# Opening loads of a spectral-filter, soft-MoE and Mish kernel: half of x on another queue, and fewer filler products

## The chip, the cores and the metric

One core of one Trainium2 chip runs the whole program. The metric is device time of one execution in microseconds (us), the median of several runs. The engines are TensorE (PE; its weight loads are listed as PEld), VectorE (DVE), ScalarE (ACT), GpSimd (POOL) and SyncE (SP). Transfers are issued by SP, ACT or POOL, each on a queue of its own (in the profile's queue table q1 is SP's, q10 ACT's, q0 POOL's), and all queues share the core's 16 DMA engines.

## What is computed

Input x is 8 sequences of 3072 rows of 256 floats. All arithmetic is float32.

```python
X = np.fft.rfft(x, axis=1)
Yr = Xr @ w_r - Xi @ w_i + b_r          # same for Yi with b_i
Yr = sign(Yr) * max(|Yr| - 0.01, 0)      # same for Yi
x = np.fft.irfft(Yr + 1j * Yi, n=3072, axis=1).reshape(8 * 3072, 256)
logits = x @ phi                          # 32 slots, 8 experts of 4
d = softmax(logits, axis=0); c = softmax(logits, axis=1)
slot_out = experts(d.T @ x)               # relu(. @ w1) @ w2 for each expert
x = c @ slot_out
h = x @ w_in
out = (h * tanh(softplus(h))) @ w_out     # Mish gate
```

## The kernel before

The program has two parts. The first, up to about 720 us, does the spectral filter and the routing for the 8 sequences (b = 0 to 7) one after another; the second does the experts and the dense Mish layer. The Fourier transform of 3072 points is split into two stages of matrix products (64 by 48 points). For b = 1 to 7 the first stage (`stage1`, L239) takes tiles `xc` of x, and its result goes through DRAM (`sdr`) and back for the second stage (`stage2`, L269). Sequence 0 is the opening and goes another way, so that nothing has to wait for DRAM: all of x[0] is loaded into one tile `x0` of 128 partitions (`load_x0`, L187 to L192), and `first(c)` for c = 0 to 3 (L194 to L211) does the first stage for 64 of the 256 columns at a time and turns the result with a DVE transpose (`bt`, L211) into the tile that `stage2` reads.

`load_x0(c)` is called for two column halves, c = 0 and 1. Each call issues four transfers: r = 0, 1 (12 of 24 rows of a partition) and h = 0, 1 (partitions 0 to 63, the lower ones, and 64 to 127, the upper ones). So x[0] comes in eight pieces of 384 KB, each of 64 partitions times 12 rows of 512 bytes. SP issues the four lower pieces, ACT the four upper ones. `first(0)` and `first(1)` read only the four pieces of c = 0, `first(2)` and `first(3)` only those of c = 1. In each, the products take lower and upper partitions in turn, so the first product needs both lower pieces and the second one both upper pieces.

The order of the work is written by hand: `at(pos, fn, ...)` puts a function at a place, and all are run in the order of their places. The opening is: `setup` (the loads, L139 to L154), 46 filler products (`fill`, L560, 64 by 64 by 64 on the constant tile `f64`, whose result nobody reads), `first(0)` and `first(1)`, 28 filler products more, `first(2)` and `first(3)`, then `load_c` and the `xc` loads of b = 1 on SP's queue, `weights("a")`, and stages of k = 0, 1, ... Each filler and each other float32 product shows as two MATMUL instructions in the profile.

`setup` issues besides x: the constant `f64` (32 KB, ACT), the first quarter of a table of cosines `tall` (432 KB, SP), the two filter matrices into `wst` (256 KB each, ACT), and, on POOL's queue, two biases (`bias`, 1 KB each, in runs of 4 bytes) and the slot vectors phi (`ph`, 32 KB, in runs of 128 bytes). `wst` is first read by `weights("a")` on ACT (L170), `bias` by `biases` on DVE (L176).

Which semaphore a transfer uses is dealt out by the framework: transfers of SP and ACT share eight of them in turn (DMAHW0 to DMAHW7 in the order listings below), and a ninth transfer waits, on its issuing queue, until the one that used the same semaphore last has landed. POOL's transfers have semaphores of their own (DMASW).

Of the kernel before, what the change touches and what calls it, by code (L numbers as in the profile page):

```python
# [70 lines left out]
def body(ctx, tc, x, w_r, w_i, b_r, b_i, phi, w1, w2, w_in, w_out, cbig, ct, out, dbg=None, stop=False):  # L71
    nc = tc.nc
# [4 lines left out]
    def at(pos, fn, *a):  # L77
        items.append((round(pos, 4), len(items), fn, a))
# [47 lines left out]
    ph = wp.tile([128, 2, NS], F32, name="ph")  # L126
    bias = wp.tile([128, 2, 2], F32, name="bias")
# [6 lines left out]
    x_t, b_t, xh_t, xl_t, yt_t, y_t, pt_t, k1_t = {}, {}, {}, {}, {}, {}, {}, {}  # L134
# [4 lines left out]
    def setup():  # L139
        nc.scalar.preload_act_table_set("natural_log_exp_and_others")  # L140
        nc.scalar.dma_start(out=f64, in_=cbig[:, 416:480])
        wst = ytp.tile([128, 6, D], F32, tag="yt", name="wst")
        k1_t["w"] = wst
        x_t[0] = opx.tile([128, 2, N2, 128], F32, name="x0")
        for c in range(2):
            load_x0(c)
        load_t(0, 0)
        nc.scalar.dma_start(out=wst[:, 0:2], in_=w_r.rearrange("(h p) e -> p h e", p=128))
        nc.scalar.dma_start(out=wst[:, 2:4], in_=w_i.rearrange("(h p) e -> p h e", p=128))
        for i, src in ((0, b_r), (1, b_i)):  # L150
            nc.gpsimd.dma_start(out=bias[:, i], in_=src.rearrange("(h p) -> p h", p=128))
        nc.gpsimd.dma_start(out=ph, in_=phi.rearrange("(h p) e -> p h e", p=128))
        nc.vector.memset(ones32, 1.0)
        x_t["bt"] = op0.tile([96, 16, D, 2], F32, name="bt0")  # L154

# [26 lines left out]
    def load_t(i, g):  # L182
        w = 8 * (96 if i else 144)
        o = NP * 144 * i + g * w
        nc.sync.dma_start(out=tall[:, o:o + w], in_=ct[:, o:o + w])

    def load_x0(c):  # L187
        src = x[0].rearrange("(p h n) d -> h p n d", h=2, n=N2)
        for r in range(2):
            for h in range(2):  # L190
                (nc.scalar if h else nc.sync).dma_start(out=x_t[0][64 * h:64 * h + 64, c, 12 * r:12 * r + 12],
                                                        in_=src[h][:, 12 * r:12 * r + 12, 128 * c:128 * c + 128])  # L192

    def first(c):  # L194
# [454 lines left out]
    def load_c0():  # L649
        for r in range(4):  # L650
            for j, n in ((0, 6), (1, 2)):
                nc.sync.dma_start(out=c0[32 * r:32 * r + 32, 6 * j:6 * j + n].bitcast(F32).rearrange("s i t -> s (i t)"),
                                  in_=c_d[0][r % 2][j][:, 0:n].rearrange("s i t -> s (i t)"))

    at(-9, setup)
    at(12.05, load_c0)
    at(-5.5, fill, 46)
    at(-0.84, biases)
    at(-4.6, weights, "a")
    at(-0.86, weights, "b")  # L660
    at(-0.85, weights, "c")
    at(-4.85, fill, 28)
    for c in range(4):
        at(-5 + 0.1 * c, first, c)
    at(-4.28, load_c)
# [486 lines left out]
```

## Time and profile before

| what | value |
|---|---|
| time, median of 3 runs | 1822.76 us (1821.73 to 1824.0) |
| profiled execution | 1821.0 us |
| its span, first to last instruction | 1819.1 us |
| PE busy | 1796.6 us, 99% of the span |
| DVE busy | 1498.4 us, 82% |
| ACT busy | 1373.1 us, 75% |
| POOL busy | 265.8 us, 15% |
| granted TensorE clock, mean | 1.000 |

The table shows that PE is busy nearly all the time. The change lies in the first 30 us of the span only, and there the views to read are those that put events in order of time: the chain of work that ended last, the timelines of the engines, the issues of transfers with their time to landing, and the stretches with the rate at which bytes moved.

### The profile page before, as it was taken

What the parts mean: (1) busy time and instruction counts of PE and PEld (TensorE: products, weight loads), DVE (VectorE), ACT (ScalarE), POOL (GpSimd) and SP (SyncE); (2) the same over time, 40 slices, a digit from 0 to 9 for tenths busy, and PEclk for the clock granted to TensorE, in tenths of its full rate; (3) what the DMA queues carried; (4) which work ended last, traced back from release to release, by engine and by line L of the source; (5) the groups of instructions that cost most, each with busy time, mean ns of one, the idle gap of its engine ahead of it and who ended that gap; (6) DMA issues with size and microseconds to landing.
All of it is one profiled execution on the core that took longest, in us unless ns stands there. A gap on an engine that the chain in (4) does not pass through costs nothing.

```text
span 1819.1 us, 32257 instructions
## 1 busy us (share of the span) xinstructions
PE 1796.6 (99%) x12522; PEld 1548.0 (85%) x12522; DVE 1498.4 (82%) x2157; ACT 1373.1 (75%) x2232; POOL 265.8 (15%) x342
## 2 busy tenths in 40 slices
PE   9999999999998999999999999999999999999998
PEld 6878788787886688888888888888888888888887
DVE  5477776766766599999999999999999999999997
ACT  4776676777673588888888888888888888888885
POOL 1334344443551000000000000000000000000000
PEclk9999999999999999999999999999999999999999
DMA  9686677567637910020020020012002002000001
GB/s 235 168 196 179 162 208 195 160 190 174 183 91 292 307 28 18 18 59 24 24 58 16 21 59 24 24 25 46 24 24 59 24 23 49 25 24 24 24 20 28
DMA packets 175048, 160.53 MB, mean 88 GB/s; under 512 B 111520, under 2 KB 144032, under 8 KB 172976
## 3 DMA queue, kind: packets, MB, share of 16 engines
q1 hardware_dynamic: 166784, 147.39, 30.7%
q0 software_dynamic: 2656, 7.90, 1.3%
q10 hardware_dynamic: 5456, 3.18, 0.8%
q8 instruction: 99, 1.62, 0.4%
q14 instruction: 53, 0.43, 0.1%
HBM read 97.08 MB, written 61.34 MB: 87 GB/s over the span
## 4 chain that ended last, share of the span: by engine, by line
PE 89%; DVE 4%; ACT 4%; issue 2%; POOL 1%; DMA 1%; ACTq 0%; DVEq 0%; POOLq 0%; SPq 0%
PE oa L1053 14%; PE ob L1053 14%; PE h L994 10%; PE l L307 8%; PE oa L1064 8%; PE oc L1064 7%; PE od L1064 7%; PE s L269 5%; PE ob L1064 4%; PE tr L362 2%; PE s L239 2%; PE pp L340 1%; PE sps L530 1%; POOL yt L329 1%; ACT cl L327 1%
## 5 line engine op out<-in xcount | busy, mean ns | idle before, releaser
L1038 DVE TENSOR_TENSOR sl<-u,sh 128x1792 fp32r<-128x1792 f32 x192 | 387.5, 2018 | 1.1 <-ACT sh L1033 1.1
L1010 ACT ACTIVATE g<-h 128x512 f32<-128x512 f32 x384 | 208.7, 596 | 144.8 <-PE h L994 141.0
L1040 DVE TENSOR_TENSOR gl<-g,gh 128x1024 fp32r<-128x1024 f32 x191 | 231.7, 1213 | 81.6 <-ACT gh L1021 81.6
L1053 PE MATMUL oa<-gh,wc 128*128 128x512 f32 x768 | 238.0, 391 | 0.0
L1053 PE MATMUL ob<-gh,wc 128*128 128x512 f32 x768 | 236.4, 389 | 0.0
L1033 ACT ACTIVATE sh<-u 128x1024 fp32r<-128x1024 f32 x192 | 201.4, 1049 | 45.3 <-DVE u L1028 45.3
L994 PE MATMUL h<-ctt,mst 128*128 128x512 f32 x736 | 229.5, 393 | 0.0
L1010 ACT ACTIVATE u<-h 128x512 f32<-128x512 f32 x384 | 207.6, 593 | 9.2
L1021 ACT ACTIVATE gh<-g 128x1024 fp32r<-128x1024 f32 x191 | 202.9, 1062 | 6.1
L1004 POOL TENSOR_TENSOR sh<-zero 128x256 fp32r<-128x256 f32 x48 | 37.8, 788 | 1133.2 <-PE ob L1064 1133.1
L327 ACT ACTIVATE cl<-p,tup 128x384 f32<-128x384 f32 x124 | 76.4, 616 | 132.9 <-DVE p L320 91.4
L1053 PEld LDWEIGHTS oa<-gh,wc 128*128 128x128 f32 x768 | 144.1, 188 | 33.9
L1053 PEld LDWEIGHTS ob<-gh,wc 128*128 128x128 f32 x768 | 144.2, 188 | 29.9
L1019 ACT ACTIVATE sh<-u 128x768 fp32r<-128x768 f32 x192 | 162.7, 847 | 9.0
L329 POOL TENSOR_TENSOR yt<-cl,p 128x384 f32<-128x384 f32 x124 | 127.6, 1029 | 279.0 <-ACT p L328 134.0
L1026 DVE TENSOR_TENSOR u<-u 128x512 f32<-128x512 f32 x192 | 150.5, 784 | 0.0
L1053 PE MATMUL oa<-gl,wc 128*128 128x512 f32 x384 | 150.0, 390 | 0.0
L1053 PE MATMUL ob<-gl,wc 128*128 128x512 f32 x384 | 149.4, 389 | 0.0
L1064 PE MATMUL od<-sh,whl 128*128 128x256 f32 x720 | 147.7, 281 | 0.0
L1064 PE MATMUL oa<-sh,whl 128*128 128x256 f32 x768 | 146.1, 283 | 0.0
L1064 PE MATMUL oc<-sh,whl 128*128 128x256 f32 x720 | 140.5, 283 | 0.0
L994 PEld LDWEIGHTS h<-ctt,mst 128*128 128x128 f32 x736 | 126.4, 190 | 14.3
(239 smaller groups left out, 3953.1 us busy)
## 6 DMA issues: line engine op xcount, KB each, us to landing
out_dram<-ot SPq DMA_DIRECT2D x380, 64.0 KB, 1.8
xc<-in_x_dram SPq DMA_DIRECT2D x84, 256.0 KB, 4.9
sdr<-a SPq DMA_DIRECT2D x84, 256.0 KB, 4.0
bt<-sdr SPq DMA_DIRECT2D x84, 256.0 KB, 5.7
ctt<-c_d SPq DMA_DIRECT2D x32, 384.0 KB, 6.9
w1t<-in_moe_w_dram SPq DMA_DIRECT2D x6, 1024.0 KB, 6.7
c_d<-chl SPq DMA_DIRECT2D x14, 384.0 KB, 3.0
w2t<-in_moe_w_dram SPq DMA_DIRECT2D x5, 1024.0 KB, 10.5
```

Source lines behind the costliest of these rows:

```text
L307: nc.tensor.matmul(full[:, 0:48 * nq].rearrange("p (q f) -> p q f", f=48), lhsT=ww[:, h, es], rhs=spec(xx, h), start=n == 0, stop=n == 5)
L329: nc.gpsimd.tensor_sub(o, cl, p)
L994: nc.tensor.matmul(h_t[p][i].rearrange("p (n t) -> p n t", n=8), lhsT=mst[:, f * 128:f * 128 + 128], rhs=(c0 if blk < 2 else ct_t[b])[:, 8 ...
L1010: nc.scalar.activation(out=v[i], in_=h[i], func=AF.Mish)
L1019: nc.scalar.activation(out=gh[:, 0:3], in_=g[:, 1:4], func=AF.Copy)
L1021: nc.scalar.activation(out=gh, in_=g, func=AF.Copy)
L1026: nc.vector.tensor_sub(g[:, 4:6], g[:, 0:1].to_broadcast([128, 2, 256]), g[:, 1:3])
L1033: nc.scalar.activation(out=gh[:, 3:7], in_=g[:, 4:8], func=AF.Copy)
L1038: nc.vector.tensor_sub(gl, g[:, 1:8], gh[:, 0:7].bitcast(F32))
L1040: nc.vector.tensor_sub(gl, g, gh.bitcast(F32))
L1053: nc.tensor.matmul(ps, lhsT=w[:, r, i, e], rhs=x[:, i], start=c == 0 and i == 0 and n == 0, stop=p == NQ - 2 and i == 1 and n == 2)
L1064: nc.tensor.matmul(ps[:, half], lhsT=w[:, r, k], rhs=y[:, x], start=False, stop=c == FAST[-1] and n == 2 and ((t, half) in (("c", 1), ("d" ...
```

## The change

The four upper pieces of x are issued by POOL instead of ACT; the two biases and the slot vectors are issued by ACT instead of POOL, behind the two filter matrices; the first group of filler products goes from 46 to 40, the second from 28 to 14. Nothing else is edited.

```diff
         nc.scalar.dma_start(out=wst[:, 2:4], in_=w_i.rearrange("(h p) e -> p h e", p=128))
         for i, src in ((0, b_r), (1, b_i)):
-            nc.gpsimd.dma_start(out=bias[:, i], in_=src.rearrange("(h p) -> p h", p=128))
-        nc.gpsimd.dma_start(out=ph, in_=phi.rearrange("(h p) e -> p h e", p=128))
+            nc.scalar.dma_start(out=bias[:, i], in_=src.rearrange("(h p) -> p h", p=128))
+        nc.scalar.dma_start(out=ph, in_=phi.rearrange("(h p) e -> p h e", p=128))
...
-                (nc.scalar if h else nc.sync).dma_start(out=x_t[0][64 * h:64 * h + 64, c, 12 * r:12 * r + 12],
+                (nc.gpsimd if h else nc.sync).dma_start(out=x_t[0][64 * h:64 * h + 64, c, 12 * r:12 * r + 12],
...
-    at(-5.5, fill, 46)
+    at(-5.5, fill, 40)
...
-    at(-4.85, fill, 28)
+    at(-4.85, fill, 14)
```

Since ACT and SP now issue other transfers, the eight shared semaphores are dealt out anew. This is the head of ACT's queue before, from the load of the constant to the first evacuation of `first(0)`; the names are those of the code, and a bracket holds the semaphores that an instruction waits on.

```order
L141 DMA f_119<-in_cbig_dram 128x64
L191 DMA x_131<-in_x_dram 64x12x128 x3
L191 DMA x_131<-in_x_dram 64x12x128 [waits DMAHW0_49]
L148 DMA wst<-in_w_r_dram 128x2x256 [waits DMAHW3_49]
L149 DMA wst<-in_w_i_dram 128x2x256 [waits DMAHW4_49]
L210 ACTIVATE a<-s_196 96x64x8 [waits PE_49]
```

The same place in ACT's queue after the change:

```order
L141 DMA f_119<-in_cbig_dram 128x64
L148 DMA wst<-in_w_r_dram 128x2x256
L149 DMA wst<-in_w_i_dram 128x2x256
L151 DMA bias<-in_b_r_dram 128x2x1
L151 DMA bias<-in_b_i_dram 128x2x1
L152 DMA ph<-in_moe_phi_dram 128x2x32
L210 ACTIVATE a<-s_190 96x64x8 [waits PE_49]
```

ACT's own transfers no longer wait for any that landed before; the filter matrices have moved from behind four pieces of x to the front.

The head of SP's queue, before and after, with the table's first two quarters (`tall`), the constants (`cb`) and the tiles `xc` of sequence 1:

```order
-L191 DMA x_131<-in_x_dram 64x12x128 x4
-L185 DMA tall<-in_ct_dram 96x1152 [waits DMAHW1_49]
-L226 DMA xc<-in_x_dram 64x1024 [waits DMAHW2_49]
+L191 DMA x_131<-in_x_dram 64x12x128 x2
+L191 DMA x_131<-in_x_dram 64x12x128 [waits DMAHW0_49]
+L191 DMA x_131<-in_x_dram 64x12x128 [waits DMAHW1_49]
+L185 DMA tall<-in_ct_dram 96x1152 [waits DMAHW2_49]
+L226 DMA xc<-in_x_dram 64x1024 [waits DMAHW3_49]
+L226 DMA xc<-in_x_dram 64x1024 [waits DMAHW4_49]
```

After the change SP's third and fourth pieces of x wait for semaphores 0 and 1, that is for its own first piece and for `f64`; before, they waited for nothing, and it was ACT's fourth piece that waited for semaphore 0. `tall` waits for w_r (semaphore 2) instead of for `f64`.

On PE the order is the same but for the two counts of filler products and the semaphores. Before, at the start of `first(0)`:

```order
L563 MATMUL fl<-f_119 64x64 x45
L203 MATMUL s_196<-x_131,f_119 32x512 [waits DMAHW3_49,DMAHW0_49]
L203 MATMUL s_197<-x_131,f_119 32x512 [waits DMAHW4_49,DMAHW2_49]
L203 MATMUL s_196<-x_131,f_119 32x512
L203 MATMUL s_197<-x_131,f_119 32x512
```

After:

```order
L563 MATMUL fl<-f_119 64x64 x39
L203 MATMUL s_190<-x_131,f_119 32x512 [waits DMAHW3_49,DMAHW0_49]
L203 MATMUL s_191<-x_131,f_119 32x512 [waits DMASW1_49,DMASW0_49]
L203 MATMUL s_190<-x_131,f_119 32x512
L203 MATMUL s_191<-x_131,f_119 32x512
```

The second product of `first(0)` now waits for POOL's first two transfers instead of ACT's.

## Rows read from the trace of the kernel before

**Rows 1.** Chain of work that ended last, start: start us, us, what.

```profile
1.95 10.90 DMA x<-in_x_dram
12.86 0.14 issue
12.99 3.65 PE s L203 x46
16.64 3.41 PE fl L563 x56
20.05 1.81 PE s L203 x13
...
23.92 1.98 DVE bt L211
25.90 0.25 issue
26.16 2.28 DVE bt L211
28.44 0.04 issue
28.48 4.20 PE s L269 x32
```

**Rows 2.** Timeline of PE's weight loads: start us, us, instruction, count [idle before].

```profile
2.60 8.00 PEld L563 LDWEIGHTS fl<-f 128*64 128x64 f32 x92 [2.60 <-DMA f<-in_cbig_dram]
11.08 0.14 PEld L203 LDWEIGHTS s<-x,f 64*32 64x32 f32 x2 [0.47 <-issue]
12.96 0.20 PEld L203 LDWEIGHTS s<-x,f 64*32 64x32 f32 x12 [1.75 <-issue]
...
16.57 3.34 PEld L563 LDWEIGHTS fl<-f 128*64 128x64 f32 x56 [0.84 <-DVE a L208]
19.98 0.14 PEld L203 LDWEIGHTS s<-x,f 64*32 64x32 f32 x2
20.69 0.28 PEld L203 LDWEIGHTS s<-x,f 64*32 64x32 f32 x12 [0.57 <-issue]
...
27.37 0.15 PEld L239 LDWEIGHTS s<-xc,f 64*64 64x64 f32 x4 [0.28 <-issue]
```

**Rows 3.** Issues in the timelines of SP, ACT and POOL: start us, us.

```profile
0.74 0.75 SPq L191 DMA_DIRECT2D x<-in_x_dram  x1
1.95 0.67 ACTq L191 DMA_DIRECT2D x<-in_x_dram  x1
2.93 1.38 SPq L191 DMA_DIRECT2D x<-in_x_dram  x1
5.70 0.60 ACTq L191 DMA_DIRECT2D x<-in_x_dram  x1
10.99 0.40 ACTq L148 DMA_DIRECT2D wst<-in_w_r_dram  x1
17.24 0.47 SPq L226 DMA_DIRECT2D xc<-in_x_dram  x1
1.29 0.89 POOL L151 DMA_DIRECT2D bias<-in_b_r_dram  x1 [0.85 <-POOLq L1132]
2.90 0.72 POOL L152 DMA_DIRECT2D ph<-in_moe_phi_dram  x1
```

**Rows 4.** The same issues, in the same order: KB, us from issue to landing.

```profile
x<-in_x_dram SPq DMA_DIRECT2D x1, 384.0 KB, 4.9
x<-in_x_dram ACTq DMA_DIRECT2D x1, 384.0 KB, 10.9
x<-in_x_dram SPq DMA_DIRECT2D x1, 384.0 KB, 14.3
x<-in_x_dram ACTq DMA_DIRECT2D x1, 384.0 KB, 14.9
wst<-in_w_r_dram ACTq DMA_DIRECT2D x1, 256.0 KB, 14.5
xc<-in_x_dram SPq DMA_DIRECT2D x1, 256.0 KB, 8.6
bias<-in_b_r_dram POOLq DMA_DIRECT2D x1, 1.0 KB, 6.5
ph<-in_moe_phi_dram POOLq DMA_DIRECT2D x1, 32.0 KB, 8.8
```

**Rows 5.** Stretches: busy us of PE, PEld, DVE, ACT, POOL, clock, DMA share, GB/s.

```profile
2.20:4.40 2.20, 1.80 (x17) 1.80 (x18) 0.00 (x0) 0.00 (x0) 1.43 (x2) 1.00 0.84 192
4.40:11.00 6.60, 6.34 (x78) 6.20 (x76) 0.00 (x0) 0.00 (x0) 0.00 (x0) 1.00 1.20 191
11.00:15.00 4.00, 3.02 (x32) 1.02 (x38) 0.69 (x1) 0.62 (x2) 0.00 (x0) 1.00 1.17 285
15.00:20.60 5.60, 5.60 (x80) 3.80 (x68) 5.19 (x3) 2.62 (x5) 0.00 (x0) 1.00 1.10 267
```

**Rows 6.** DMA queues, 15 to 17 us: packets, MB, share of 16 engines.

```profile
q1 hardware_dynamic: 291, 0.43, 81.8%
q10 hardware_dynamic: 287, 0.15, 31.9%
```

**Rows 7.** Stretches, filler products only: busy us of PE and PEld, clock, DMA.

```profile
2.60:8.30 5.70, 5.70 (x53) 5.70 (x54) 1.00 1.12 200
8.30:10.80 2.50, 2.44 (x42) 2.30 (x40) 1.00 1.23 194
```

**Rows 8.** Whole run: POOL's queue (packets, MB, share) and POOL's issues (to landing).

```profile
q0 software_dynamic: 2656, 7.90, 1.3%
wf_d<-ws POOLq DMA_DIRECT2D x12, 256.0 KB, 3.5
win_d<-cvs POOLq DMA_DIRECT2D x16, 128.0 KB, 2.3
```

**Rows 9.** Timelines of DVE and POOL, opening and about 472 us.

```profile
15.82 4.50 DVE L211 STREAM_TRANSPOSE bt<-a 96x2048 f32<-96x2048 f32 x2
471.53 0.96 DVE L436 TENSOR_TENSOR lg<-lg,cm 128x768 f32<-128x768 f32 x1
471.88 0.68 POOL L621 DMA_DIRECT2D wf_d<-ws  x1 [0.41 <-POOL ws L620]
```

## Prediction

> **What bounds the kernel now.** The table of busy time says that PE works 99% of the span, so what PE is late with in the opening is late at the end, unless something absorbs it. I read the chain of work that ended last first [rows 1]. Its opening is x: it waits 10.90 us on a piece of x, runs `first(0)` and `first(1)` (3.65 us), the second filler group (3.41 us), then `first(2)` and `first(3)`, and the last DVE transposes release `stage2` at 28.48. The timeline of PE's weight loads shows what the chain hides [rows 2]. The first filler group ends at 10.60, the first product of `first(0)` starts at 11.08, but the second only at 12.96. The second filler group ends just before 19.98; there one product of `first(2)` starts, and the rest only at 20.69. These two waits end with landings: ACT's second piece, issued at 1.95, lands 10.9 later, at 12.85; ACT's fourth, issued at 5.70, lands 14.9 later, at 20.60 [rows 3, 4]. I call these points T0 and T1. So the second filler group isn't the bound, though the chain lists it: when it is done, x is still missing.
>
> Why T1 is late: ACT's fourth piece was issued only at 5.70, when SP's first had landed (0.74 + 4.9 = 5.64) [rows 3, 4]; they share a semaphore. It then travels beside SP's `tall`. From 15 to 17 us both queues got equally many packets (291 and 287), but 0.43 MB against 0.15 [rows 6]: ACT's rows of 512 bytes lose against SP's 4.6 KB rows. The rate of all queues is 191 GB/s from 4.4 to 11.0 and 285 from 11.0 to 15.0 [rows 5]; the change of rate comes near 11.7, where POOL's last small load lands (2.90 + 8.8) [rows 3, 4].
>
> **The change part by part.** After T1 nothing is edited: from 20.69 to 28.48 lie the products, evacuations and transposes of c = 2 and 3. So the gain is what T1 moves, if PE gets there in time and the other feeders come no later.
>
> T0. Ahead of it must land `f64` (33 KB), four pieces of x (4 x 393 = 1573 KB) and, since the filter matrices now come first on ACT's queue, 524 KB of those: 2130 KB. The stretches up to 20.6 give 192 x 2.2 + 191 x 6.6 + 285 x 4.0 + 267 x 5.6 = 4318 KB in 18.4 us, 235 GB/s [rows 5]. From 2.2 us this makes T0 = 2.2 + 2130 / 235 = 11.3; at 191 it is 13.4, at 285 it is 9.7. I take the mean rate, since both halves of the old opening return: small loads at first, none later.
>
> T1. Four more pieces make 3703 KB, the slot vectors 3736 KB. Of `tall` (442 KB), which stands behind SP's fourth piece, between nothing and all goes along with POOL's last one. That gives 2.2 + 15.9 = 18.1 and 2.2 + 17.8 = 20.0; I take the middle, 19.0, against 20.69: **1.7 us earlier**. With the packets of equal count [rows 6], POOL's pieces should not starve: POOL's queue averages 7.90 MB / 2656 = 3.0 KB a packet [rows 8], against 512 bytes on ACT's. SP's halves pay for that while POOL's pass, which the sum of bytes holds already.
>
> The issue on POOL. No row shows it for a load of this size. Its issues of 1 and 32 KB took 0.89 and 0.72 us; the first landed 6.5 us after issue, at 7.8 [rows 3, 4]. Lower bound: four issues of 0.9 from 1.29 end at 4.9, before SP's second piece could have landed, and cost nothing. Upper bound: one piece at a time. Stores of 128 and 256 KB took 2.3 and 3.5 us [rows 8], 1.2 for each 128 KB more, so 4.7 for 384 KB; the first would land at 7.8 + 3 x 1.2 = 11.4, the fourth at 11.4 + 3 x 4.7 = 25.5. I take the lower, since POOL has nothing else queued before 39 us and DMA time is full anyway, and keep the upper as a rival.
>
> SP's pieces three and four now wait for SP's first (5.64 at the latest rate): they wait behind the second in the same queue anyway, so nothing. ACT's six issues take some 0.4 each (w_r's row) and end near 3.5, long before the first evacuation: nothing; before, two of them stood in the queue until 13. The biases and the slot vectors, 33 KB in tiny rows, stay in the DMA engines whichever queue issues them. Either they slow the others as before (191 GB/s, the slow end above) or they come after x's first pieces. They are read after 35 us.
>
> Filler. Before the clock's step 53 instructions took 5.70 us, 108 ns each, after it 42 took 2.50, 60 ns [rows 7]. Twelve instructions less end the first group 0.7 earlier, at 9.9, and T0 at 11.3 hides it. `first(0)` and `first(1)` then end at 15.0; 28 instructions of 0.06 end at 16.7, before T1 = 19.0. So both cuts are worth nothing in the sum; they only matter if x comes faster. If PE's clock should fall in the gaps (1.4 and 2.3 us, where the longest gap before was 1.75 on the weight loads and the clock stayed at 2.4 GHz), it is a rival.
>
> Other feeders. The last `xc` tile needed lands at 17.24 + 8.6 = 25.8 and is used at 27.37 [rows 2 to 4], 1.5 us of slack; after the change its issue waits for a bias instead of x, so it can come earlier. w_r landed at 25.5, at the moment of its use; it is now far ahead. So 1.7 us pass to 28.48.
>
> The sum: the profiled execution took 1821.0 us; 1821.0 - 1.7 = 1819.3. It lies 1.76 below the median of the three runs, so on the median 1822.76 - 1.7 = **1821.1 us**. What a measurement of this kernel can tell from no change is 0.2%, 3.65 us, and the forecast lies within it.
>
> **The rivals.**
>
> *Faster.* Without POOL's small loads all goes at 285 GB/s: T0 = 9.7 and T1 between 2.2 + 13.1 = 15.3 and 16.9. PE then sets the time: filler to 9.9, `first` to 13.6, 0.8 until a bank is free [rows 2], filler to 16.1. T1 is 16.1 to 16.9, 3.8 to 4.6 earlier: about 1818.6. For it speaks that the rate rose when those loads were done; against it, that they still have to pass.
>
> *POOL's pieces one after another.* T1 = 25.5, 4.8 later: 1827.6, slower. It decides if the pieces land more than (20.7 - 11.4) / 3 = 3.1 us apart. The 3.5 us for 256 KB speak for it, that those had nothing queued behind them against it. The Trainium skill's page "DMA: Bandwidth & Descriptors" (Terms) says that descriptors issued by GpSimd are 16 bytes and are written to rings in SBUF; the kernel's scratch of 1024 bytes (L1132) would hold 64 of them, my estimate from that page, and a piece has 48 rows for each of 16 DMA engines, so that a second one wouldn't fit beside the first.
>
> *DVE holds POOL up.* If POOL can't prepare the fourth piece while DVE transposes, it comes after the second transpose, which ended 20.32 - 12.96 = 7.36 after T0 [rows 2, 9]: 18.7, and 4.7 later lands at 23.4, 2.7 late: 1825.5. Against it: at 471.88 POOL's issue took its usual 0.68 us under a DVE operation from SBUF to SBUF [rows 9]. The page "SBUF — State Buffer" (SBUF: two separate sides) states the rule, that GpSimd can't write descriptors while DVE runs an operation that takes their shared port; the one row here doesn't agree.
>
> *Nothing moves.* All queues use the same 16 DMA engines and T1 is set by bytes: 1822.8, within 0.5. The page "DMA: Bandwidth & Descriptors" (Rules for kernel authors) says just this, that spreading transfers over SP, ACT and GpSimd doesn't help bandwidth; the rise from 191 to 285 GB/s on the same queues shows that there is room.
>
> *The clock falls in a gap.* PE ran 5.7 us at half speed at the start; half of that is lost again, 2.85, less the 1.7: 1823.9.
>
> **How the numbers follow.** Forecast 0.42, faster 0.15, one after another 0.13, DVE 0.10, nothing 0.15, clock 0.05. Faster by over 0.2%: 0.15 and 0.02 of the forecast's fast end, 0.17; slower by over 0.2%: 0.13 and 0.02 of the DVE rival, 0.15; within: 0.68. The range reaches from the fast rival to past the DVE one, 1818.3 to 1826.0, and leaves out most of the one-after-another case.
>
> **What would show it.** The second weight load group of `first(0)` near 11.3 and that of `first(2)` near 19.0; `stage2` after the transposes near 26.8; POOL's four issues together by 6 us (if they stretch past 10, its pieces go singly); over 235 GB/s between 2.2 and 19. A second product of `first(2)` after 20.7, or filler products and L203 at 108 ns instead of 60 after 8.3, would make the prediction wrong.

## The result, and the profile after

The changed kernel takes 1840.24 us (median; 1839.89 to 1840.83), the kernel before beside it 1823.25 (1821.73 to 1824.0): a ratio of 1.0091, with a 95% interval of [1.0078, 1.0103]. So it is slower by 17.0 us; the forecast was 1821.1, in a range that ended at 1826.0.

The chain of work that ended last in the changed kernel, its start (start us, us, what), is the answer to [rows 1]:

```profile
1.30 0.93 POOL x L191
2.23 7.07 issue
9.30 0.78 POOL x L191
10.08 9.80 issue
19.88 0.76 POOL x L191
20.64 10.04 issue
30.68 5.53 DMA x<-in_x_dram
36.21 0.14 issue
36.35 6.39 PE s L203 x46
42.73 2.17 PE s L269 x16
```

Before, the opening of the chain was one piece of x and then PE's own work. Now 36 us of it belong to POOL: an issue, a wait in which the view finds nothing that POOL waits for ("issue"), the next issue, and so on four times, and then the last piece's transfer.

The timeline of PE's weight loads after (start us, us, instruction, count [idle before]), which answers to [rows 2]:

```profile
2.54 7.11 PEld L563 LDWEIGHTS fl<-f 128*64 128x64 f32 x80 [2.54 <-DMA f<-in_cbig_dram]
12.55 0.14 PEld L203 LDWEIGHTS s<-x,f 64*32 64x32 f32 x2 [2.89 <-issue]
19.68 0.24 PEld L203 LDWEIGHTS s<-x,f 64*32 64x32 f32 x12 [7.00 <-issue]
...
25.81 1.71 PEld L563 LDWEIGHTS fl<-f 128*64 128x64 f32 x28 [0.84 <-ACT a L210]
27.59 0.14 PEld L203 LDWEIGHTS s<-x,f 64*32 64x32 f32 x2
36.31 0.24 PEld L203 LDWEIGHTS s<-x,f 64*32 64x32 f32 x12 [8.59 <-issue]
...
46.71 3.99 PEld L269 LDWEIGHTS s<-tall,bt 96*128 96x128 f32 x32 [0.81 <-DVE bt L211]
```

T0 is 19.68 instead of 12.96, T1 36.31 instead of 20.69. In both `first(0)` and `first(2)` the first product, which needs only SP's pieces, stands there 7 to 9 us before the second: what is late is POOL's half alone. T1 is 15.6 us later. From T1 to the second batch of `stage2` it now takes 46.71 - 36.31 = 10.40 us instead of 7.79, 2.6 more. Together that is 18.2 us, and the span has grown by 1837.8 - 1819.1 = 18.7: the opening holds all but 0.5 us of it.

The 2.6 us are PE's clock. Stretches of the changed kernel (busy us of PE, PEld, DVE, ACT and POOL, granted clock, DMA share, GB/s), to be held against [rows 5]:

```profile
4.40:11.00 6.60, 5.40 (x66) 5.26 (x64) 0.00 (x0) 0.00 (x0) 0.78 (x1) 1.00 1.17 203
11.00:15.00 4.00, 1.01 (x2) 0.14 (x2) 0.00 (x0) 0.00 (x0) 0.00 (x0) 0.95 1.22 176
15.00:20.60 5.60, 0.89 (x11) 0.31 (x17) 0.00 (x0) 0.00 (x0) 0.72 (x1) 0.50 1.05 213
30.00:36.00 6.00, 0.00 (x0) 0.00 (x0) 0.00 (x0) 0.00 (x0) 0.75 (x1) 0.64 0.78 167
36.00:43.00 7.00, 6.65 (x48) 2.00 (x49) 1.85 (x1) 3.41 (x7) 0.00 (x0) 0.58 0.00 0
```

After one product at 12.55 PE stood idle (1.01 us busy of the four from 11 to 15), and the clock is 0.50 in the next stretch; it was idle from 30 to 36 and the clock is 0.64 there and 0.58 in the stretch of `first(2)` and `first(3)`. 46 instructions of L203 take 6.39 us there (the chain above) and took 3.65 before [rows 1]: 2.7 for the late part. The DMA engines meanwhile were busy: up to 20.6 us their share is as high as before. But little of what they moved was what PE waited for: from 10 to 15 us it was mostly SP's pieces of x, two of them for c = 1, and from 15 to 36 us SP's queue (the table, `xc` and the constants) moved 3.24 MB, POOL's 1.16.

### The profile page after: what moved, and what is told of

It is laid out like the page before. It is cut to its first block, busy times and chain, and to the rows that moved or that the text cites. A ratio compares the mean times of both kernels' runs of the same rounds, so it can differ in the third digit from the quotient of the medians.

```text
span 1837.8 us, 32178 instructions
## 1 busy us (share of the span) xinstructions
PE 1799.7 (98%) x12482; PEld 1545.7 (84%) x12482; DVE 1499.4 (82%) x2157; ACT 1373.6 (75%) x2232; POOL 266.9 (15%) x343
## 4 chain that ended last, share of the span: by engine, by line
PE 87%; ACT 4%; DVE 3%; issue 3%; POOL 1%; DMA 0%; DVEq 0%; ACTq 0%; POOLq 0%; SPq 0%
PE oa L1053 14%; PE ob L1053 14%; PE h L994 10%; PE l L307 8%; PE oa L1064 8%; PE oc L1064 7%; PE od L1064 7%; PE s L269 5%; PE ob L1064 4%; PE tr L362 2%; PE s L239 2%; PE pp L340 1%; PE sps L530 1%; POOL yt L329 1%; ACT cl L327 1%
```

## Experiments

Each is compared with the kernel before, run beside it on the same chip (its median there was 1824.0 to 1824.2).

### Which part of the change costs it

**Only x's upper half on POOL's queue.** The small loads and the filler stay as before.

```diff
# against the kernel before
-                (nc.scalar if h else nc.sync).dma_start(...)   # load_x0
+                (nc.gpsimd if h else nc.sync).dma_start(...)
```

> The kernel before with only x's four upper pieces on POOL's queue; the small loads stay on POOL, which issues them ahead of x or between, and both filler groups keep 46 and 28 products. Theory A (POOL's room for one piece alone makes the loss): the pieces land one after another, the last at 36 to 39 us, stage2's second batch starts at 45 to 49 and the time is 1838 to 1842, like the changed kernel. Theory B (a good part of the loss comes from the other two parts, the small loads on ScalarE or the shorter filler): the last piece lands before 32 and the time is below 1834.

Measured: 1841.69 us, ratio 1.0092 [1.0078, 1.0106]. POOL's timeline in this run:

```profile
1.29 0.93 POOL L191 DMA_DIRECT2D x<-in_x_dram  x1 [0.84 <-POOLq L1132]
9.34 0.78 POOL L191 DMA_DIRECT2D x<-in_x_dram  x1 [7.12 <-issue]
21.27 0.76 POOL L191 DMA_DIRECT2D x<-in_x_dram  x1 [11.15 <-issue]
32.67 0.76 POOL L191 DMA_DIRECT2D x<-in_x_dram  x1 [10.64 <-issue]
37.89 0.73 POOL L151 DMA_DIRECT2D bias<-in_b_r_dram  x1 [4.46 <-issue]
38.61 0.72 POOL L151 DMA_DIRECT2D bias<-in_b_i_dram  x1
```

This part alone makes the whole loss, and the last piece lands at 37.6. The bias loads at the end give a plain comparison: the second follows the first at once, while a piece of x makes whatever is behind it wait, even the small bias load at 37.89.

**Only the small loads on ACT's queue.**

```diff
# against the kernel before; the same two lines in the change
-            nc.gpsimd.dma_start(out=bias[:, i], ...)
+            nc.scalar.dma_start(out=bias[:, i], ...)
-        nc.gpsimd.dma_start(out=ph, ...)
+        nc.scalar.dma_start(out=ph, ...)
```

> The kernel before with one of the change's three parts: the biases and slot vectors are issued by ScalarE behind the filter matrices, x and the filler stay as before. Theory A (the small loads at the head slow the other queues, 191 against 285 GB/s in the profile before): without them ahead of x the rate between 2.2 and 11 us is well over 230 GB/s, the second product of first(0) starts at 10 to 11 instead of 12.96, the rest of first(2) at 17 to 18.5 instead of 20.69, and the time is 1820 to 1822. Theory B (the rate of the first 11 us belongs to the start of the x transfers themselves, whatever POOL loads): the rate stays near 190, the second product of first(0) at 12.5 to 13.5, first(2) near 20.7, and the time stays within 1 us of before.

Measured: 1827.19 us, ratio 1.0011 [1.0002, 1.002]. Two stretches of this run, columns as above:

```profile
2.20:11.00 8.80, 8.38 (x93) 8.12 (x94) 0.00 (x0) 0.00 (x0) 0.00 (x0) 1.00 1.10 197
11.00:15.00 4.00, 3.35 (x43) 1.11 (x46) 1.29 (x2) 0.00 (x0) 0.00 (x0) 1.00 1.17 290
```

With no small load ahead of x the rate is 197 GB/s up to 11 us and 290 after, as it was with them (191 and 285, [rows 5]). The step of the rate that I had read as their end has another cause, and of the rate the second theory holds. What that cause is was not tried. Of the time it doesn't hold: it had 1 us, and this part alone costs 2.0 us by the ratio (0.4 to 3.6 by the interval). In the profile of this run PE waits 3.33 us ahead of `first(2)`, which starts at 22.76 and then takes 6.64 us for its 48 instructions; the chain puts that wait down to a bias load, which is now on ACT's queue. Why this costs time was not tried either. The costs of the three parts don't add up: together they cost what x's half costs alone.

**Only the shorter filler.**

```diff
# against the kernel before; the same two lines in the change
-    at(-5.5, fill, 46)
+    at(-5.5, fill, 40)
-    at(-4.85, fill, 28)
+    at(-4.85, fill, 14)
```

> The kernel before with 40 and 14 filler products and nothing else changed. Theory of the prediction: both groups are hidden by the wait for x; T0 and T1 stay at 12.96 and 20.69 us, the time within 1 us of before. Rival (the fillers hold the clock): it falls in the longer gaps, one or both pairs of first() take some 6 us instead of 3.65, up to 2.7 us slower.

Measured: 1826.58 us, a ratio of 1.0010 [1.0001, 1.0019], some 1.8 us (one of the ten executions took 1960.26 us, and the ratio leaves it out). PE's timeline (start us, us, instruction, count [idle before]):

```profile
10.54 1.02 PE L203 MATMUL s<-x,f 64*32 64x512 f32 x2 [1.23 <-DMA x<-in_x_dram]
13.05 5.34 PE L203 MATMUL s<-x,f 64*32 64x512 f32 x46 [1.49 <-DMA x<-in_x_dram]
...
22.93 5.34 PE L203 MATMUL s<-x,f 64*32 64x512 f32 x46 [1.79 <-issue]
```

T0 is where it was, but the 46 instructions behind it take 5.34 us instead of 3.65, and so do those behind T1: with the first group shorter, PE stood idle 1.23 us and then, but for one product, 1.49 more, and the granted clock from 11 to 15 us is 0.80 instead of 1.00. At T0 the filler bought that clock: with 46 products the group took 3.65 us in both profiles of the kernel before. At T1 that isn't shown: the kernel before, run once more, has 5.34 there with 28 products, and a run with 14 has 3.65 (the last two runs below). And PE still waits 1.79 us for x at T1, so that what was lost at T0 is made good there. That the 1.8 us are the clock is likely, not shown.

**The longer filler back in the changed kernel, and a much longer one.** Both are edits of the two counts only: to 46 and 28, and to 120 and 110.

> The changed kernel with 46 and 28 filler products again. Theory of the prediction: the filler is hidden by the wait for x, so T0 and T1 stay at 19.7 and 36.3 us and the time at 1840 us within 1 us. Rival (the cut of the filler lets the clock fall): L203's products of each pair of first() take 3.65 us again instead of 6.2 to 6.4, stage2 starts 2.7 us earlier, 1837.5 us.

> The changed kernel with 120 and 110 filler products, enough to keep PE at work until each time x lands. Theory clock (the low clock of the two pairs of first() costs what it shows): T0 and T1 stay at 19.7 and 36.3 us, the clock stays at 2.4 GHz, L203's products take 3.65 us each time, stage2 starts at 44.0 instead of 46.7 us, 1837.5 us. Rival (its cost is hidden by ACT's evacuations or DVE's transposes): stage2 moves by under 1 us, 1840 us.

Measured: 1840.53 us, ratio 1.0088 [1.0073, 1.0103], with the old counts, and 1841.11, 1.0097 [1.0080, 1.0114], with the long ones: neither gives anything back. With 46 and 28 PE still idles 6.85 and 6.75 us ahead of the two points, and both groups of L203 take 5.9 us. The long filler does hold the clock (PE's timeline of that run):

```profile
21.13 3.64 PE L203 MATMUL s<-x,f 64*32 64x512 f32 x46 [1.61 <-DMA x<-in_x_dram]
...
29.68 9.38 PE L563 MATMUL fl<-f 128*64 128x64 f32 x158 [1.15 <-issue]
38.98 3.65 PE L203 MATMUL s<-x,f 64*32 64x512 f32 x48
```

The products take 3.65 us again and `stage2`'s second batch comes 46.77 - 38.98 = 7.8 after their start, as before. So the 2.6 us are the clock. The time of 1837.5 that the theory had from them didn't come. The filler was itself too long: it ended at 39.0, 1.5 us after the last piece had landed in this run (32.62 + 4.8 = 37.4). The other 1.1 us are too little to be seen here.

### Why POOL's pieces come one after another

**Twice the room for POOL's descriptors.** One number is edited (L1132).

```diff
# against the changed kernel
-    nc = _bacc.Bacc("TRN2", ..., dynamic_dma_scratch_size=1024)
+    nc = _bacc.Bacc("TRN2", ..., dynamic_dma_scratch_size=2048)
```

> The changed kernel with 2048 bytes a partition for POOL's descriptors instead of 1024. In the changed kernel POOL issues its four pieces at 1.30, 9.30, 19.88 and 30.68 us, each 0.3 us after the one before has landed. Theory ring (POOL waits for room for its descriptors): 64 descriptors for each DMA engine hold one piece (48 rows and an end), 128 hold two. The first two pieces are issued by 2.5 us, the third 0.3 us after the first lands, the fourth after the second; T0 at 10 to 14 us, T1 at 20 to 26 us, time 1824 to 1831 us. Theory one-at-a-time (POOL lets only one of its transfers be under way, whatever the room): issues as in the changed kernel, T1 36 us, 1840 us.

Measured in one run: 1830.68 us. POOL's timeline:

```profile
1.29 1.69 POOL L191 DMA_DIRECT2D x<-in_x_dram  x2 [0.84 <-POOLq L1132]
9.08 0.76 POOL L191 DMA_DIRECT2D x<-in_x_dram  x1 [6.11 <-issue]
13.21 0.75 POOL L191 DMA_DIRECT2D x<-in_x_dram  x1 [3.37 <-issue]
```

Two pieces are issued at once, the third when the first has landed (1.29 + 7.5 = 8.8), and so on. T1 is 26.69, just past the 20 to 26 that the theory had, and some 9.5 us of the loss are gone.

**Pieces half as large.** POOL issues eight of 192 KB. A whole piece is 64 partitions by 12 rows, 48 rows for each of the 16 DMA engines; a half is 24.

```diff
# against the changed kernel, in load_x0
-                (nc.gpsimd if h else nc.sync).dma_start(out=x_t[0][..., 12 * r:12 * r + 12], ...)
+                for q in range(2 if h else 1):   # rows 12r + 6q to 12r + 6q + 6 for the upper half
+                    (nc.gpsimd if h else nc.sync).dma_start(out=x_t[0][..., n], ...)
```

> The changed kernel with each of POOL's four pieces cut in two of 6 rows a partition (24 rows and an end for each DMA engine). Theory ring: two of the eight are under way at a time; the second is issued right behind the first, the third 0.3 us after the first lands. With 5 to 8 us from issue to landing T1 is 22 to 34 us, time 1826 to 1839 us. Theory one-at-a-time: eight in a row, each 5 to 9 us, T1 41 to 73 us, time 1845 to 1877 us.

Measured in one run: 1839.36 us. The head of POOL's timeline:

```profile
1.29 1.50 POOL L193 DMA_DIRECT2D x<-in_x_dram  x2 [0.84 <-POOLq L1134]
7.83 0.66 POOL L193 DMA_DIRECT2D x<-in_x_dram  x1 [5.04 <-issue]
11.49 0.65 POOL L193 DMA_DIRECT2D x<-in_x_dram  x1 [3.00 <-issue]
```

Two halves fit at a time, a third doesn't. So it isn't a rule of one transfer at a time; it is room. Counted in rows, two halves (48 an engine) fit into 1024 bytes and three (72) don't; into 2048 two whole pieces (96) fit and three (144) don't. Counted in bytes moved it would be 384 and 768 KB; the next run tells the two apart. The Trainium skill, page "DMA: Bandwidth & Descriptors" (Terms), says that a descriptor is 16 bytes and that GpSimd writes them to rings in SBUF; 1024 bytes would hold 64 of them, an estimate from that page, and 2048 would hold 128. Both lie between the bounds that these runs show. The time is no better: 1839.36 and T1 at 35.31 lie past the theory's ranges (up to 1839 and 34). All but the first and the last half took 8.2 to 9.3 us from issue to landing, against 10.3 and 10.5 of whole pieces in the changed kernel, so that two at a time gained next to nothing.

**Whole rows.** If rows count, longer rows must help with the same bytes. Two pieces of 768 KB for each half, in rows of 12 KB (4 rows an engine a piece) instead of 512 bytes; the filler is 62 and 2, since `first(0)` then needs all of x. Once with POOL as in the change, and once, as a base, with ACT as before.

```diff
# against the changed kernel (and, with nc.scalar, against the kernel before)
-        x_t[0] = opx.tile([128, 2, N2, 128], F32, name="x0")
+        x_t[0] = opx.tile([128, N2, D], F32, name="x0")
...
-                (nc.gpsimd if h else nc.sync).dma_start(out=x_t[0][64 * h:64 * h + 64, c, 12 * r:12 * r + 12],
-                                                        in_=src[h][:, 12 * r:12 * r + 12, 128 * c:128 * c + 128])
+                (nc.gpsimd if h else nc.sync).dma_start(out=x_t[0][64 * h:64 * h + 64, 12 * r:12 * r + 12],
+                                                        in_=src[h][:, 12 * r:12 * r + 12])
```

> The kernel before (upper half of x on ACT, small loads on POOL), but x in whole rows: the tile x0 has 24 rows of 256 columns a partition and each queue loads two pieces of 768 KB, in runs of 12 KB instead of 512 bytes; 62 and 2 filler products, since all of x lands at one time. Theory rows (the runs of 512 bytes limit the rate to 190 to 285 GB/s and lose against longer ones): all of x has landed by 13 to 15 us, first(0) to first(3) follow each other, stage2 starts at 25 to 27 instead of 28.48 us, 1820 to 1822 us. Rival (bytes set the time): the last piece lands near 17 us, T0 moves from 13 to 17, stage2 to 29, 1824 us or more.

> The changed kernel, upper half of x on POOL, with x in whole rows as in e8_rows and 62 and 2 filler products: POOL issues two pieces of 64 runs of 12 KB, some dozen descriptors for each DMA engine instead of 48 for each of four. Theory ring: both are issued back to back by 3 us and land by 11 to 16 us; first(0) starts there, 1820 to 1825 us, the 17 us are gone with POOL still issuing. Rival (POOL's queue is slow whatever it carries): the second piece is issued at 9 us or later and lands at 19 us or later, 1828 us or more.

Measured: 1826.85 us with ACT, ratio 1.0015 [1.0006, 1.0024]: longer rows alone don't speed the opening up. T0, which then needs all of x, is 19.50, and the theory that the rows' length holds the opening back missed. With POOL 1828.39, 1.0026 [1.0017, 1.0035]. POOL's timeline:

```profile
1.29 1.22 POOL L190 DMA_DIRECT2D x<-in_x_dram  x2 [0.84 <-POOLq L1130]
```

Both issues stand back to back, they land 16.4 us after issue (the mean of the two), and all of x is there at 21.0, where the changed kernel had it at 36.3. Two pieces of 768 KB fit into the room that held one of 384, so the room is not counted in bytes moved; rows fit all these runs. With the same bytes on the same queue all but 4 to 5 of the 17 us are gone; between POOL and ACT it is 1.5 us, and the two intervals overlap. Theory ring was right on the issues only: it had all landed by 16 and 1820 to 1825 us, while the landing and the time came out as its rival had them.

**Less traffic beside POOL's pieces.** What decides how long one piece takes? The loads of the first four `xc` tiles, the second part of the table and the constants `cb` go from SP's queue to ACT's, where they stand behind the evacuations of `first(3)`.

```diff
# against the changed kernel
-        nc.sync.dma_start(out=cb, ...)
+        nc.scalar.dma_start(out=cb, ...)
-        nc.sync.dma_start(out=tall[:, o:o + w], ...)
+        (nc.scalar if (i, g) == (0, 1) else nc.sync).dma_start(out=tall[:, o:o + w], ...)
-            nc.sync.dma_start(out=t[64 * h:64 * h + 64], ...)
+            (nc.scalar if b == 1 and i < 4 else nc.sync).dma_start(out=t[64 * h:64 * h + 64], ...)
```

> The changed kernel with the loads that SP issues behind x and the first quarter of tall (four xc tiles of sequence 1, the second quarter, the constants) moved to ACT's queue behind the evacuations of first(3), so that they start after the last piece of x has landed. Theory traffic (POOL's pieces take 10 us from issue to landing because other queues' transfers run beside them, and 5.5 when they don't): pieces 3 and 4 take 5 to 6.5 us each, T1 27 to 31 instead of 36.3 us; the time itself gains less or nothing, since the xc tiles come later. Rival (a piece of 768 runs takes POOL 10 us by itself): as in the changed kernel, 10 us for the third.

Measured in one run: 1839.92 us. POOL's timeline, and then the last piece's entry in the list of issues (KB, us to landing):

```profile
9.03 0.78 POOL L191 DMA_DIRECT2D x<-in_x_dram  x1 [6.81 <-issue]
19.27 0.76 POOL L191 DMA_DIRECT2D x<-in_x_dram  x1 [9.46 <-issue]
24.43 0.75 POOL L191 DMA_DIRECT2D x<-in_x_dram  x1 [4.40 <-issue]
```

```profile
x<-in_x_dram POOLq DMA_DIRECT2D x1, 384.0 KB, 4.9
```

The third and the fourth piece, now with little beside them, take 4.9 us each; the second, beside SP's pieces and the table, still takes 9.9. T1 comes at 29.47, 6.8 earlier than in the changed kernel. The time doesn't follow, because the `xc` loads that were moved away are then late themselves: `stage1` waits for them at 40.04, and `stage2`'s second batch comes at 45.22.

### A try at a faster opening, and the kernel before once more

ACT's fourth piece of x was the late one before. Here it goes on SP's queue, ahead of the table, with the second filler group at 14.

```diff
# against the kernel before
-                (nc.scalar if h else nc.sync).dma_start(...)   # load_x0
+                (nc.scalar if h and not (c and r) else nc.sync).dma_start(...)
...
-    at(-4.85, fill, 28)
+    at(-4.85, fill, 14)
```

> An attempt at a faster opening: the kernel before, but x's last upper piece (the one that was issued at 5.70 and travelled beside the table) goes on SP's queue ahead of the table, so that SP issues five pieces and ScalarE three, and the second filler group has 14 products instead of 28. Theory A (the last piece was late since it was issued late and shared the engines with the table's longer rows): the rest of first(2) starts at 17.5 to 18.5 instead of 20.69, stage2's second batch near 26.3 instead of 28.48, and the time is 1 to 2.5 us below before. Theory B (bytes set the end, or the shorter filler lets the clock fall): first(2) starts at 20 or later, or its products take over 5 us instead of 3.65, and the time is the same as before or up to 2 us more.

> The kernel before once more, for how far the marks of the opening vary from one profiled execution to another: if they are steady, the second product of first(0) starts within 0.5 us of 12.96, the rest of first(2) within 0.7 of 20.69, stage2's second batch within 1 of 28.48, and the products of first take 3.6 to 3.7 us each time. If they vary more, differences of 1 to 2 us between single profiles of the other runs mean nothing by themselves.

Measured for the five pieces on SP: 1823.57 us, ratio 0.9997 [0.9988, 1.0006], no difference. T1 is 20.91: the piece was issued at 4.54 and took 16.3 us, as if it had stayed where it was. The gain of the first theory isn't there, and the marks and the time lie in the ranges of the second; that it is bytes that set the end is not shown by it. No version here beats the kernel before. The clock stayed up in this run, with 14 filler products in the second group.

The kernel before, run once more, gave 1827.63 us in that profiled execution, and the marks of its opening are PE's (start us, us, instruction, count [idle before]):

```profile
12.94 3.65 PE L203 MATMUL s<-x,f 64*32 64x512 f32 x46 [1.26 <-DMA x<-in_x_dram]
...
24.37 5.34 PE L203 MATMUL s<-x,f 64*32 64x512 f32 x46 [3.40 <-issue]
```

T0 is steady (12.91 and 12.96), T1 isn't: 24.34 instead of 20.69, with `stage2`'s second batch at 33.68 instead of 28.48. ACT's fourth piece took 18.3 us to land this time, 17.2 in the run with the shorter filler, and 14.9 in the profile that I predicted from [rows 4]. So differences of up to 3.7 us in T1 between single profiles mean nothing, and the ratios decide; the 15.6 us of the changed kernel are far outside.

## Why the prediction was wrong

**The bound.** Read rightly: T0 and T1, both landings of x's upper half, set the opening, and all that was lost was lost through them. That nothing changes behind T1 held in everything but the clock.

**The step that failed: the issue on POOL.** I had two bounds, four issues by 4.9 us or one piece at a time, and took the lower, "since POOL has nothing else queued before 39 us". That is no argument about what an issue itself waits for. The rows for it were of 1 and 32 KB, and neither fills anything. I put the term at nothing. The four issues came at 1.30, 9.30, 19.88 and 30.68, all but the first 0.3 us after the landing of the piece before, and T1 was 36.31 instead of 19.0. The reason against my choice stood in the prediction itself, in the rival *one after another*: room for 64 descriptors by its estimate, 48 for a piece. The doubled room, the halves and the whole rows show that it is this room. It should have had the larger chance. The trace of before could not show the effect, since no load of many rows was on POOL's queue early.

**The rival's price was too low as well.** It had 4.7 us a piece, from stores of 128 and 256 KB, and 25.5 for T1. Here are the four issues of the changed kernel, in order (KB, us to landing):

```profile
x<-in_x_dram POOLq DMA_DIRECT2D x1, 384.0 KB, 7.7
x<-in_x_dram POOLq DMA_DIRECT2D x1, 384.0 KB, 10.3
x<-in_x_dram POOLq DMA_DIRECT2D x1, 384.0 KB, 10.5
x<-in_x_dram POOLq DMA_DIRECT2D x1, 384.0 KB, 5.5
```

7.7 + 10.3 + 10.5 + 5.5 and the start and the gaps make 36.2. With little beside it a piece takes 4.9 us, close to the price I had; with SP's pieces, the table and `xc` beside it, twice that. I used a row from a quieter part of the program (the one store of [rows 9] lies in a stretch with a DMA share of 0.50, from 470 to 480 us) for a stretch whose share is above 1. The Trainium skill's fit on "DMA: Bandwidth & Descriptors" (Anatomy of one DMA), 2.0 us and the bytes at 436 GB/s, would give 2.9 us for a piece, an estimate from that page; even the undisturbed 4.9 doesn't agree with it.

ACT's pieces had not landed faster: 10.9 and 14.9 us from issue to landing [rows 4], against 5.5 to 10.5 on POOL. But up to four of them were under way at a time. What the change took away was the overlap, and time to landing doesn't show that; the distance between landings does: 2.7 to 5.0 us on ACT's queue before, 5.8 to 10.8 on POOL's.

**T0 by bytes.** 2130 KB at 235 GB/s should have made T0 11.3. The rate was lower (203 and 176 GB/s in the stretches above), and already the first product of `first(0)`, which waits for SP's first two pieces alone, ran at 12.55: without POOL's wait T0 would have missed 11.3 too. The larger error is that the sum took what the engines move to be what is waited for. SP's queue had no such block and went on to its pieces for c = 1. From 10 to 14 us, with POOL's second piece issued at 9.30, these are the queues that moved anything (packets, MB, share of 16 engines), and POOL's isn't among them; SP's 0.5 KB a packet are rows of x:

```profile
q1 hardware_dynamic: 1263, 0.63, 111.1%
q10 hardware_dynamic: 602, 0.04, 14.6%
```

SP's queue, nearly alone with such rows, moved 176 GB/s from 11 to 15 us, where SP's and ACT's together had moved 285 before [rows 5]. The mean rate had both queues in it.

**The filler.** That "both cuts are worth nothing" was wrong for the kernel before: alone they cost some 1.8 us there (0.2 to 3.5 by the interval), likely by the clock. I had counted the group's end against T0 and T1 and put the clock among the rivals as a thing of the new gaps. In the changed kernel the cuts don't matter, since the waits are so long that the old counts don't cover them either.

**The clock.** The rival had 2.85 us for half of what the start loses; it came, as 2.6, but as a consequence of the late pieces and on top of them. The half speed at the start that the price came from was read from the time of an instruction (108 and 60 ns); the granted clock in [rows 7] is 1.00 in both stretches.

**What held.** ACT's six issues cost nothing, and w_r landed 5.3 us after its issue instead of 14.5. `xc` was early. SP's pieces for c = 1 were not late: the first product of `first(2)` ran at 27.59, straight behind the filler, 8.7 us before the second.

**The other rivals.** *DVE holds POOL up* is not what made the loss: DVE did nothing between 1.0 and 21.74 us, and the second piece, issued at 9.30, landed at 19.6 all the same. The row that the prediction held against it says little: DVE ran a TENSOR_TENSOR there and no transpose, and no run here shows which operations of DVE take the shared port. *Faster* rested on the small loads being what slowed the first 11 us, and they aren't. *Nothing moves* would need the same transfers under way at the same time. The Trainium skill's rule behind it, "DMA: Bandwidth & Descriptors" (Rules for kernel authors), that spreading transfers over the queues doesn't help, holds in what it says (no gain here); that it can cost 17 us the rule doesn't say.

**The base.** The profile that the sum started from had the earliest T1 of those seen (20.69; 22.9 and 24.3 in others with the same loads). A gain of 1.7 us would have lain within that scatter.

## What to carry to other kernels

Before a load goes on POOL's queue, count its rows for each DMA engine against the room for POOL's descriptors: if two don't fit, POOL stands still until the first has landed, and everything behind it on that queue too; longer rows took some 12 of the 17 us away here, twice the room 9.5. Price a transfer by a row from as busy a stretch as the one it goes to, and compare queues by the distance between landings, not by the time from issue to landing. Filler that ends before the wait does can still be of use, if it keeps PE's clock at 2.4 GHz; measure the cut by itself.

## What the runs showed of the hardware

POOL's room in this kernel: at 1024 bytes one piece of 48 rows an engine, or two of 24, or two of 4 rows of 12 KB; at 2048 two of 48. An issue that waits for room shows in the chain and the timeline as "issue", with no releaser, and ends some 0.3 us after the earlier landing.

A POOL piece of 384 KB, alone on its queue, takes 4.8 to 5.5 us with little beside it and 7.4 to 11.9 beside what SP and ACT issue, and part of that is a wait before anything moves: issued at 9.30, it had moved no packet by 14. Whether POOL's descriptors are written late there, or fetched late, was not settled.

The granted clock fell to 1.2 GHz (0.50) in the stretch from 15 to 20.6 us, after PE had been busy for 1.01 us of the four before, and the 46 instructions from 19.71 on took 6.17 us instead of 3.65. In one execution of the kernel before, they took 5.34 after a wait of 3.40 us.

The rate of the opening, about 190 to 200 GB/s up to 11 us and 280 to 290 from there to 15, is the same in the kernel before with and without the small loads at its head.
